# Column 0 of the attention tile: VectorE casts become ScalarE copies, and the first units are issued in another order

## The chip, the core and the metric

The kernel runs on one core of a Trainium2 chip. A core has five engines that run their own instruction queues side by side and meet at semaphores: TensorE (PE, matrix multiplies; PEld is its weight load), VectorE (DVE), ScalarE (ACT), GpSimd (POOL) and SyncE (SP, which here only issues DMA transfers). The metric is the device time of one execution in microseconds. Before the change three runs took 1192.21, 1198.12 and 1201.44 us, so the median is 1198.12 us.

## The reference, cut to what matters

```python
def mab(q, kv):                      # B, N, C = 4, 12608, 128; 32 inducing rows
    s = scale * (q @ kv.transpose(0, 2, 1))
    a = np.exp(s - s.max(-1, keepdims=True))
    a /= a.sum(-1, keepdims=True) + 1e-09
    return a @ kv
h = mab(I, x)                        # 32 rows attend to all of x
x = mab(x, h)                        # all of x attends to the 32 rows of h
x_prev = shift_by_one_row(x)         # first row zero
k = np.maximum((mu_k*x + (1-mu_k)*x_prev) @ w_k, 0.0)       # d_ff = 1024
r = sigmoid((mu_r*x + (1-mu_r)*x_prev) @ w_r)
out = r * (k*k @ w_v)
```

The shift by one row is what the change touches: every stretch of tokens needs the last token of the stretch before it.

## The kernel before, in words

Each of the 4 batches is cut into 6 blocks of 2048 tokens and a tail of 320. A block is 4 groups of 512 tokens. The expensive part, the channel mix, runs in **units**: one group has 4 units, each of 256 of the 1024 hidden columns, so there are 400 units in all. A unit is

- `up` (L882, PE): six matmuls of R (attention weights of the group) with W into a bank pair `ps_a`, of which there are two;
- `square` (L892, DVE): the relu out of `ps_a` into `k_t`; then L900 and L901 (ACT): the square, once rounded into `kh`, once in full into `k_t`; then L904 (POOL): `kl` = the rest;
- `down` (L916, PE): six matmuls of kh and kl with the two halves of w_v, issued four units behind its `up`.

The main loop takes two units at a time. At the group's end DVE multiplies by the gate (L921) and transposes (L931), and SP stores. `zgate` (L865, PE) and L868 (ACT) compute the gate.

The attention is woven in between the units. A table of events (`at(n, f)`, run at the end of the loop step that holds unit n; `soon(n, f)` runs earlier, between the `up`s and the squares of that step) says what is issued when, and that order is the order of every engine's queue. `stage_a` of the next batch: scores (L406, PE, bank `pb_a`), its maximum and exponential, `hmm` (L473, PE, also into `pb_a`) and `acc` (L486 or L488, DVE), which empties `pb_a`; the next block's scores can only be written into `pb_a` when acc has read it. `stage_b` of the next block of this batch: scores (L640, PE), a softmax on DVE and ACT, and its result as a high and a low part in the tile `ahl` (128 partitions x 2 x 513): `high` is L680 (ACT), `low` is L683 (DVE). `ahl` has four strips of 32 partitions, one per group; column 0 of a strip must hold the last column of the strip before it. That is `joins`: three copies of 32x2 elements from `ahl` itself (L693) and one from the R of the previous block (L695; at a batch's first block it is a memset, L697). `spread` (L706 and L707, SP) then copies `ahl` by DMA into four R tiles, and waits for joins. There are 23 such blocks (a batch's tail has no joins, and the first block of batch 0 is made otherwise). Two of them, the second block of batch 0 and the first of batch 1, are on a shorter schedule (`quick`).

The first block of batch 0 goes group by group in `start`: softmax parts (`sc`, `tu`, `mx`, `df`, `ex`, `nm`), then `high` (`hi0` to `hi3`: ACT L812) and `put` (`put0` to `put3`): transposes on PE (L817), the high part on ACT (L823), the low part on DVE (L824), then the copy of rows 0 to 31 to rows 32 to 63, one column on. For group 0 that copy is two casts on ACT and two on DVE (L829); for groups 1 to 3 it is a POOL memset (L832) and two SP DMAs (L834) and two small ones for column 0 (L620), which need the previous group's R and the L834 pair. The parts of units 3 to 8 are held back to named steps by `finish`.

Of the kernel before, what the change touches and what calls it, by code (L numbers as in the profile page):

```python
# [8 lines left out]
F32 = mybir.dt.float32  # L9
# [10 lines left out]
def kernel(  # L20
# [11 lines left out]
    nc = tc.nc  # L32
    B, N, C = x.shape
    M = inducing.shape[0]
    F = w_k.shape[1]
    P = 128
    Q = 4
    FC = F // P
    G = 512
# [24 lines left out]
    HP = P // 2  # L64
# [557 lines left out]
    def stage_b(b, j, at, t, quick=False):  # L622
# [3 lines left out]
        S = batches[b]  # L626
# [55 lines left out]
        def low():  # L682
            nc.vector.tensor_tensor(out=L["a"][:, 1, 1:w + 1], in0=L["aT"],  # L683
                                    in1=L["a"].bitcast(F32)[:, 0, 1:w + 1], op=ALU.subtract)
            if full:
                joins()

        def joins():
            A = L["a"]
            for i in range(Q):  # L690
                dst = A[M * i:M * (i + 1), :, 0:1]
                if i > 0:
                    nc.vector.tensor_copy(out=dst, in_=A.bitcast(F32)[M * (i - 1):M * i, :, G:])  # L693
                elif j > 0:
                    nc.vector.tensor_copy(out=dst, in_=S.R[j * Q - 1].bitcast(F32)[:M, :, G - 1:G])  # L695
                else:
                    nc.vector.memset(dst.bitcast(F32), 0.0)  # L697

# [46 lines left out]
        at(t + 6, back)  # L745
        at(t + 7, high)
        at(t + 9, low)
        for i in range(Q):
            at(t + 10 + i, lambda i=i: spread(i))

    def stage_b_head(gs):
# [3 lines left out]
        S = batches[0]  # L755
# [50 lines left out]
        def place(k):  # L806
            g = gs[k]
            X = {}

            def high():  # L810
                X["a"] = scratch[:, g % 2].rearrange("p (k q m) -> p k q m", k=Q, q=Q)
                nc.scalar.copy(out=X["a"], in_=L["q", k].unsqueeze(2).broadcast_to([P, Q, Q, M]))  # L812

            def put():
                ps = pb_tile("a")
                for c in range(Q):
                    nc.tensor.transpose(out=ps[:, c * P:(c + 1) * P], identity=ident,  # L817
                                        in_=X["a"][:, c].rearrange("p q m -> p (q m)"))
                rows(S, g)
                R = S.R[g]  # L820
                src = ps.rearrange("r (s p) -> r p s", p=M)
                hi, lo = (R[:, x, :G].rearrange("r (p s) -> r p s", p=M) for x in range(2))
                nc.scalar.copy(out=hi, in_=src)  # L823
                nc.vector.tensor_tensor(out=lo, in0=src, in1=hi.bitcast(F32), op=ALU.subtract)  # L824
                if g == 0:
                    halo(S, g)
                    for x, copy in enumerate((nc.scalar.copy, nc.vector.tensor_copy)):
                        for p in (0, HP):
                            copy(out=R[p + M:p + 2 * M, x, 1:G], in_=R.bitcast(F32)[p:p + M, x, :G - 1])  # L829
                    return  # L830
                flat = R.bitcast(F32).rearrange("p x g -> p (x g)")
                nc.gpsimd.memset(flat[:, G:G + 1], 0.0)  # L832
                for p in (0, HP):
                    nc.sync.dma_start(out=flat[p + M:p + 2 * M, 1:2 * G + 1], in_=flat[p:p + M, :2 * G])  # L834
                halo(S, g)
            return high, put
# [118 lines left out]
    def finish(n):  # L955
        return lambda: run(held.pop(n))
# [172 lines left out]
    def at(n, f, place=1):  # L1129
        events.setdefault(n, ([], [], []))[place].append(f)  # L1130
# [4 lines left out]
    def start():  # L1135

        part0, pl0 = stage_b_head([0, 1])
        part1, pl1 = stage_b_head([2, 3])
        sc0, tu0, mx0, df0, ex0, nm0 = part0([0])
        sc1, tu1, mx1, df1, ex1, nm1 = part0([1])  # L1140
        sc2, tu2, mx2, df2, ex2, nm2 = part1([0, 1])
        (hi0, put0), (hi1, put1) = pl0

        def bank():
            return pv.tile([P, G], F32, name="ps_v")

        wa, wb, wg = (wpart(c, bank) for c in (0, 1, None))
        assert F // G == 2
        S = batches[0]
        scores_1, settle_1, home_1 = sooner[2:]  # L1150
        rexp, rman, rsign, rjoin = conv["r", 0]
        run([sc0, gates, rexp, sc1, tu0, mx0, df0, ex0, wa[0], scores_1, tu1, nm0, wa[1],
             hi0, wa[2], rman, mx1, df1, rsign, rjoin, put0, ex1, wb[0], wb[1], wg[0], settle_1, wg[1],
             *vlow, nm1, wb[2], hi1])
        for n, f in ((0, wg[2]), (1, put1), (1, sc2)):
            soon(n, f)
        (hi2, put2), (hi3, put3) = pl1
        for n, f in ((1, tu2), (1, mx2), (1, df2), (1, ex2), (1, home_1), (2, nm2), (2, hi2), (2, hi3),
                     (3, finish(3)), (4, finish(4)), (5, finish(5)), (5, put2)):
            at(n, f)  # L1160
        soon(4, lambda: units[0][0].gate_tile())
        for f in (lambda: units[0][0].zgate(first=True, hold=sig), lambda: run(reversed(sig)),
                  finish(6), finish(7)):
            at(7, f, 0)
        at(7, put3)
# [87 lines left out]
```

## Time and profile before

| what | value |
|---|---|
| profiled execution, its own time | 1201.99 us |
| span, first to last instruction | 1199.1 us, mean granted TensorE clock 0.958 |
| busy PE / DVE / ACT / POOL | 1100.9 / 1011.2 / 913.1 / 955.6 us |
| L904 POOL, kl | x399, 935.7 us |
| L892 DVE, k_t | x400, 465.5 us |
| L693 + L695 DVE, joins | x69 + x20, 92.6 + 43.0 us |

The span is what the trace covers; 2.9 us of the execution lie outside it. Busy times of engines overlap, so their sum says nothing; what counts is where PE stands still and on whom it waits. The granted clock is 1.00 where TensorE runs at 2.4 GHz throughout and 0.5 where it runs at 1.2 GHz, the two levels it has.

### The profile page before, as it was taken

Reading aid. Unit: us, or ns where it says so; the run is one execution under the profiler, and the core shown is the slowest. Engines: PE = TensorE matmul, PEld = TensorE weight load, DVE = VectorE, ACT = ScalarE, POOL = GpSimd, SP = SyncE. Lnnn points to the kernel's source line nnn. Section 1 sums busy time; section 2 is a strip of 40 time slices with the busy share of each in tenths; the row PEclk is TensorE's granted clock in tenths of the full one; section 3 lists DMA queues with packets and bytes.
Section 4 is the critical chain, followed back from the end, with each engine's and each line's share of the span. In section 5 each row is a group of like instructions: output and inputs, shape, how many; then the busy total and the mean of one; then the engine's idle time right before and its main releaser. Section 6 shows DMA issues by size and latency. Waiting matters only on the chain.

```text
span 1199.1 us, 18674 instructions
## 1 busy us (share of the span) xinstructions
PE 1100.9 (92%) x6493; PEld 759.7 (63%) x6493; DVE 1011.2 (84%) x1343; ACT 913.1 (76%) x1065; POOL 955.6 (80%) x431
## 2 busy tenths in 40 slices
PE   8789889889999988989999889988999999998998
PEld 6466556557676655657666557655766766666776
DVE  7869999887799989987688999998768798898765
ACT  7677677668787776767887677865887888787896
POOL 4378678679888876877887778866988889898997
PEclk9899899889999989999999999998999999998999
DMA  8118557764156687575117567785322345444122
GB/s 327 45 53 199 126 128 176 186 155 86 18 118 161 150 193 176 138 184 122 32 20 173 141 154 171 176 194 135 74 33 40 77 88 106 89 96 93 34 39 39
DMA packets 250973, 142.22 MB, mean 119 GB/s; under 512 B 220000, under 2 KB 221184, under 8 KB 248576
## 3 DMA queue, kind: packets, MB, share of 16 engines
q1 hardware_dynamic: 248048, 140.68, 51.2%
q8 instruction: 51, 0.84, 0.3%
q10 hardware_dynamic: 2832, 0.36, 0.2%
q14 instruction: 42, 0.34, 0.1%
HBM read 45.89 MB, written 43.65 MB: 75 GB/s over the span
## 4 chain that ended last, share of the span: by engine, by line
PE 66%; DVE 21%; issue 5%; DMA 3%; ACT 3%; SPq 1%; POOL 1%; DVEq 0%; ACTq 0%; POOLq 0%
PE ps_v L916 34%; PE ps_a L882 22%; DVE k_t L892 8%; PE ps_v L865 4%; DVE ahl L695 2%; DVE xs L370 2%; DVE ahl L693 2%; PE pb_a L406 2%; DVE oT L921 1%; ACT kh L900 1%; PE pb_a L473 1%; DVE ot L931 1%; DMA xt<-xd 1%; DMA R<-R 1%; ACT k_t L901 1%
## 5 line engine op out<-in xcount | busy, mean ns | idle before, releaser
L904 POOL TENSOR_TENSOR kl<-k_t,kh 128x1024 fp32r<-128x1024 f32 (+1 forms) x399 | 935.7, 2377 | 212.2 <-ACT k_t L901 190.0
L892 DVE TENSOR_SCALAR k_t<-ps_a 128x1024 f32<-128x1024 f32 (+1 forms) x400 | 465.5, 1197 | 68.4 <-PE ps_a L882 67.6
L900 ACT ACTIVATE kh<-k_t 128x1024 fp32r<-128x1024 f32 (+1 forms) x375 | 388.9, 1037 | 162.1 <-DVE k_t L892 122.4
L901 ACT ACTIVATE k_t<-k_t 128x1024 f32<-128x1024 f32 (+1 forms) x400 | 419.1, 1048 | 45.8 <-DVE kh L897 33.8
L882 PE MATMUL ps_a<-R,W 64*128 64x512 f32 (+1 forms) x2400 | 358.3, 428 | 31.6 <-DVE k_t L892 24.9
L882 PEld LDWEIGHTS ps_a<-R,W 64*128 64x128 f32 x2400 | 222.9, 195 | 160.2 <-issue 68.5
L916 PE MATMUL ps_v<-kh,wvh 128*128 128x512 f32 (+1 forms) x800 | 259.7, 406 | 0.0
L916 PE MATMUL ps_v<-kh,wvl 128*128 128x512 f32 (+1 forms) x800 | 247.5, 391 | 0.0
L916 PE MATMUL ps_v<-kl,wvh 128*128 128x512 f32 (+1 forms) x800 | 244.9, 387 | 0.0
L916 PEld LDWEIGHTS ps_v<-kh,wvh 128*128 128x128 f32 x800 | 144.7, 191 | 61.8 <-issue 18.6
L916 PEld LDWEIGHTS ps_v<-kh,wvl 128*128 128x128 f32 x800 | 151.2, 190 | 32.8
L916 PEld LDWEIGHTS ps_v<-kl,wvh 128*128 128x128 f32 x800 | 150.6, 189 | 32.2
L868 ACT ACTIVATE rT<-ps_v 128x512 f32<-128x512 f32 (+1 forms) x99 | 57.8, 584 | 51.8 <-PE ps_v L865 51.8
L921 DVE SCALAR_TENSOR_TENSOR oT<-rT,ps_v 128x512 f32<-128x512 f32 (+1 forms) x100 | 66.4, 664 | 34.9 <-PE ps_v L916 34.3
L693 DVE CAST ahl<-ahl 32x2 fp32r<-32x2 f32 x69 | 92.6, 1342 | 1.7
L865 PE MATMUL ps_v<-R,W 128*128 128x512 f32 (+1 forms) x198 | 76.5, 469 | 0.0
L406 PE MATMUL pb_a<-xt,indT 128*32 128x512 f32 x112 | 23.0, 909 | 53.4 <-DVE acc L488 38.9
L931 DVE STREAM_TRANSPOSE ot<-oT 128x512 f32<-128x512 f32 (+1 forms) x100 | 69.1, 691 | 0.1
L865 PEld LDWEIGHTS ps_v<-R,W 128*128 128x128 f32 x198 | 31.9, 203 | 38.9 <-issue 38.9
L370 DVE STREAM_TRANSPOSE xs<-xb 128x512 f32<-128x512 f32 x68 | 45.5, 688 | 0.2
L695 DVE CAST ahl<-R 32x2 fp32r<-32x2 f32 x20 | 43.0, 2149 | 0.0
L406 PEld LDWEIGHTS pb_a<-xt,indT 128*32 128x32 f32 x112 | 2.7, 126 | 63.4 <-DVE acc L488 45.0
(215 smaller groups left out, 555.7 us busy)
## 6 DMA issues: line engine op xcount, KB each, us to landing
R<-ahl SPq DMA_DIRECT2D x184, 128.2 KB, 2.6
R<-ahl SPq DMA_DIRECT2D x184, 128.1 KB, 2.5
out_dram<-ot SPq DMA_DIRECT2D x184, 128.0 KB, 3.5
xb<-in_x_dram SPq DMA_DIRECT2D x18, 1024.0 KB, 8.5
xd<-xs SPq DMA_DIRECT2D x34, 512.0 KB, 3.2
xt<-xd SPq DMA_DIRECT2D x68, 256.0 KB, 5.4
kh<-in_x_dram SPq DMA_DIRECT2D x4, 512.0 KB, 6.2
kl<-in_x_dram SPq DMA_DIRECT2D x4, 512.0 KB, 9.5
```

Of the source, the lines that this page charges most:

```text
L370: nc.vector.transpose(out=xs.rearrange("p (s q) -> p s q", q=M), in_=S.xb[j][:, :, M * c:M * (c + 1)])
L693: nc.vector.tensor_copy(out=dst, in_=A.bitcast(F32)[M * (i - 1):M * i, :, G:])
L695: nc.vector.tensor_copy(out=dst, in_=S.R[j * Q - 1].bitcast(F32)[:M, :, G - 1:G])
L865: nc.tensor.matmul(out=ps[:, :w], lhsT=S.W[0][:, F:WF], rhs=R[:, x, :w], start=(x == 0), stop=(x == 1))
L882: nc.tensor.matmul(out=ps[:, c, :w], lhsT=S.W[wt][hs, cs], rhs=R[hs, x, :w], start=(n == 0), stop=(n == 2))
L892: nc.vector.tensor_scalar(out=k, in0=ps[:, :, :w], scalar1=0.0, scalar2=None, op0=ALU.max)
L900: nc.scalar.activation(out=kh, in_=k, func=AF.Square)
L901: nc.scalar.activation(out=k, in_=k, func=AF.Square)
L904: eng.tensor_tensor(out=kl[:, :, a:z], in0=k[:, :, a:z], in1=kh.bitcast(F32)[:, :, a:z], op=ALU.subtract)
L916: nc.tensor.matmul(out=self.v, lhsT=wt[:, fc, :], rhs=kk[:, c, :], start=(fc == 0 and n == 0), stop=(fc == FC - 1 and n == 2))
L921: nc.vector.scalar_tensor_tensor(out=self.oT, in0=self.rT, scalar=1.0, in1=self.v, op0=ALU.add, op1=ALU.mult)
L931: nc.vector.transpose(out=ot[:, o:o + w], in_=self.oT)
```

## The change

Four edits.

1. `joins` uses `nc.scalar.copy` instead of `nc.vector.tensor_copy`, and on the full blocks that are not `quick` it is issued one event later than `low` (on `quick` blocks still right behind it). The memset stays on DVE.
2. `put0`: the copy of the low part of group 0 by one column becomes two SP DMAs instead of two DVE casts. The high part stays on ACT.
3. `start`: put1 moves from ahead of the squares of units 0 and 1 to behind them; the scores of groups 2 and 3 (`sc2`) and their softmax move from step 0 to step 2.
4. `nm2` and `hi2` move from step 2 to step 4, `hi3` to step 5, put2 ahead of `finish(5)`.

```diff
-            if full:
+            if full and quick:
                 joins()
@@ joins
-                    nc.vector.tensor_copy(out=dst, in_=A.bitcast(F32)[M * (i - 1):M * i, :, G:])
+                    nc.scalar.copy(out=dst, in_=A.bitcast(F32)[M * (i - 1):M * i, :, G:])
                 elif j > 0:
-                    nc.vector.tensor_copy(out=dst, in_=S.R[j * Q - 1].bitcast(F32)[:M, :, G - 1:G])
+                    nc.scalar.copy(out=dst, in_=S.R[j * Q - 1].bitcast(F32)[:M, :, G - 1:G])
@@ stage_b
         at(t + 9, low)
+        if full:
+            at(t + 10, joins)
@@ put, g == 0
-                    for x, copy in enumerate((nc.scalar.copy, nc.vector.tensor_copy)):
-                        for p in (0, HP):
-                            copy(out=R[p + M:p + 2 * M, x, 1:G], in_=R.bitcast(F32)[p:p + M, x, :G - 1])
+                    for p in (0, HP):
+                        nc.scalar.copy(out=R[p + M:p + 2 * M, 0, 1:G], in_=R.bitcast(F32)[p:p + M, 0, :G - 1])
+                        nc.sync.dma_start(out=R.bitcast(F32)[p + M:p + 2 * M, 1, 1:G],
+                                          in_=R.bitcast(F32)[p:p + M, 1, :G - 1])
@@ start
-        for n, f in ((0, wg[2]), (1, put1), (1, sc2)):
+        for n, f in ((0, wg[2]), (2, sc2), (4, nm2), (4, hi2)):
             soon(n, f)
-        for n, f in ((1, tu2), (1, mx2), (1, df2), (1, ex2), (1, home_1), (2, nm2), (2, hi2), (2, hi3),
-                     (3, finish(3)), (4, finish(4)), (5, finish(5)), (5, put2)):
+        for n, f in ((1, put1), (1, home_1), (2, tu2), (2, mx2), (2, df2), (2, ex2),
+                     (3, finish(3)), (4, finish(4)), (5, put2), (5, finish(5)), (5, hi3)):
             at(n, f)
```

The changed file's line numbers are 2 or 3 higher than those of before behind `spread` (L693, L695, L706 and L707 keep theirs): L892 there is L895, L900 and L901 are L903 and L904, L904 (POOL) is L907, L921 is L924, L931 is L934, L832 is L835.

On DVE, at the end of the second block of batch 0, before:

```order
L931 STREAM_TRANSPOSE ot<-oT 128x512
L683 TENSOR_TENSOR ahl<-pb_b,ahl 128x512
L695 CAST ahl<-R 32x2
L693 CAST ahl<-ahl 32x2 x3
L892 TENSOR_SCALAR k_t<-ps_a 128x1024 x2
L370 STREAM_TRANSPOSE xs<-xb 128x512 x2
```

and on DVE at the same place after the change:

```order
L934 STREAM_TRANSPOSE ot<-oT 128x512
L683 TENSOR_TENSOR ahl<-pb_b,ahl 128x512
L895 TENSOR_SCALAR k_t<-ps_a 128x1024 x2
L370 STREAM_TRANSPOSE xs<-xb 128x512 x2
L924 SCALAR_TENSOR_TENSOR oT<-rT,ps_v 128x512
```

The four casts between the subtraction (L683) and the next two relus are gone from DVE's queue. On ACT at that place after the change:

```order
L903 ACTIVATE kh<-k_t 128x1024
L904 ACTIVATE k_t<-k_t 128x1024
L695 CAST ahl<-R 32x2
L693 CAST ahl<-ahl 32x2 x3
L871 ACTIVATE rT<-ps_v 128x512
L903 ACTIVATE kh<-k_t 128x1024
```

They stand there behind a unit's two squares and ahead of the gate's tanh (L871, before L868) and the next squares.

On POOL at the start of the unit loop (kl of units 0, 1, ... and the memsets of put1, put2 and put3), before:

```order
L179 TENSOR_TENSOR wvl<-ot,wvh 128x512 x2
L832 MEMSET R 128x1
L904 TENSOR_TENSOR kl<-k_t,kh 128x1024 x6
L832 MEMSET R 128x1
L904 TENSOR_TENSOR kl<-k_t,kh 128x1024 x2
L832 MEMSET R 128x1
```

and on POOL after the change:

```order
L179 TENSOR_TENSOR wvl<-ot,wvh 128x512 x2
L907 TENSOR_TENSOR kl<-k_t,kh 128x1024 x2
L835 MEMSET R 128x1
L907 TENSOR_TENSOR kl<-k_t,kh 128x1024 x3
L835 MEMSET R 128x1
L907 TENSOR_TENSOR kl<-k_t,kh 128x1024 x3
```

The first memset, on which put1's DMAs wait, now stands behind the kl of units 0 and 1; the second stands behind five kl instead of six.

## Rows read from the trace of the kernel before

**Rows 1.** First part of the page: busy time, share of span, instructions.
```profile
PE 1100.9 (92%) x6493; PEld 759.7 (63%) x6493; DVE 1011.2 (84%) x1343; ACT 913.1 (76%) x1065; POOL 955.6 (80%) x431
```

**Rows 2.** Waits of PE: who waited for whom, us in total, times, longest.
```profile
PE pb_a L406 <- DVE acc L488: 38.9, 9, 5.6
PE ps_a L882 <- DVE k_t L892: 24.9, 16, 3.2
PE pb_a L406 <- DVE acc L486: 14.5, 3, 4.9
```

**Rows 3.** Groups of instructions by line and form: busy us, mean ns, idle before.
```profile
L892 DVE TENSOR_SCALAR k_t<-ps_a 128x1024 f32<-128x1024 f32 x384 | 453.1, 1213 | 66.4 <-PE ps_a L882 65.7
...
L693 DVE CAST ahl<-ahl 32x2 fp32r<-32x2 f32 x69 | 92.6, 1342 | 1.7
...
L695 DVE CAST ahl<-R 32x2 fp32r<-32x2 f32 x20 | 43.0, 2149 | 0.0
...
L440 ACT ACTIVATE alpha<-mkr 128x1 f32<-128x1 f32 x15 | 4.2, 277 | 0.0
```

**Rows 4.** Instructions on tile R, 40 to 90 us: ns min/median/max, first and last start.
```profile
L829 ACT CAST R<-R x2: 612/614/617, 43.3 to 43.9; 32x511 fp32r<-32x511 f32 x2
...
L829 DVE CAST R<-R x2: 1234/1328/1423, 43.5 to 44.8; 32x511 fp32r<-32x511 f32 x2
```

**Rows 5.** Timeline of one block's end: start, us, engine, line, count, idle before.
```profile
449.81 1.83 DVE L695 CAST ahl<-R 32x2 fp32r<-32x2 f32 x1
...
451.68 4.91 DVE L693 CAST ahl<-ahl 32x2 fp32r<-32x2 f32 x3
...
451.82 4.74 POOL L904 TENSOR_TENSOR kl<-k_t,kh 128x1024 fp32r<-128x1024 f32 x2 [0.20 <-PE ps_a L882]
...
456.29 1.04 PE L640 MATMUL pb_b<-xt,hT 128*32 128x512 f32 x8
...
459.71 1.06 ACT L900 ACTIVATE kh<-k_t 128x1024 fp32r<-128x1024 f32 x1 [5.98 <-DVE k_t L892]
...
461.88 0.31 DVE L488 SCALAR_TENSOR_TENSOR acc<-acc,alpha,pb_a 128x128 f32<-128x128 f32 x1
...
462.24 1.57 PE L406 MATMUL pb_a<-xt,indT 128*32 128x512 f32 x8 [4.91 <-DVE acc L488]
```

**Rows 6.** Windows from joins to joins: length, busy PE PEld DVE ACT POOL, clock.
```profile
127.72:166.70 38.98, 34.16 (x200) 22.71 (x199) 35.45 (x46) 26.91 (x32) 28.59 (x13) 0.91 0.62 149
...
488.10:522.46 34.36, 31.82 (x200) 21.69 (x199) 32.78 (x45) 26.92 (x32) 28.58 (x13) 1.00 0.78 182
...
778.05:816.28 38.23, 33.35 (x200) 22.23 (x199) 35.20 (x46) 26.92 (x32) 28.57 (x13) 0.96 0.77 170
...
995.88:1025.66 29.78, 29.78 (x160) 20.70 (x159) 25.82 (x33) 26.20 (x29) 28.24 (x13) 1.00 0.55 107
1025.66:1059.45 33.79, 31.61 (x160) 21.59 (x159) 30.30 (x34) 26.08 (x29) 28.82 (x13) 0.95 0.39 78
```

**Rows 7.** Timeline of the first units, 36 to 75 us.
```profile
45.82 0.10 POOL L832 MEMSET R<- 128x1 f32 x1
...
46.25 2.07 PE L882 MATMUL ps_a<-R,W 64*128 64x512 f32 x7 [0.93 <-DVE R L829]
...
50.80 1.25 SPq L834 DMA_DIRECT2D R<-R  x2
...
51.99 0.96 PE L882 MATMUL ps_a<-R,W 64*128 64x512 f32 x6 [1.91 <-DVE k_t L892]
...
55.98 3.18 PE L882 MATMUL ps_a<-R,W 64*128 64x512 f32 x12 [1.21 <-DMA R<-R]
...
72.97 0.47 PE L882 MATMUL ps_a<-R,W 64*128 64x512 f32 x1 [2.97 <-DMA R<-R]
```

**Rows 8.** Timeline behind the first joins, 96 to 98 us.
```profile
96.94 1.47 PE L882 MATMUL ps_a<-R,W 64*128 64x512 f32 x5 [2.58 <-DVE k_t L892]
...
97.30 0.82 PEld L882 LDWEIGHTS ps_a<-R,W 64*128 64x128 f32 x5 [0.17 <-DMA R<-ahl]
```

More of the change, by code (lines that the diff above doesn't have):

```diff
@@ L1142, in start @@
         (hi0, put0), (hi1, put1) = pl0
+        (hi2, put2), (hi3, put3) = pl1
         def bank():
@@ L1154, in start @@
              *vlow, nm1, wb[2], hi1])
-        for n, f in ((0, wg[2]), (1, put1), (1, sc2)):
+        for n, f in ((0, wg[2]), (2, sc2), (4, nm2), (4, hi2)):
             soon(n, f)
-        (hi2, put2), (hi3, put3) = pl1
-        for n, f in ((1, tu2), (1, mx2), (1, df2), (1, ex2), (1, home_1), (2, nm2), (2, hi2), (2, hi3),
-                     (3, finish(3)), (4, finish(4)), (5, finish(5)), (5, put2)):
+        for n, f in ((1, put1), (1, home_1), (2, tu2), (2, mx2), (2, df2), (2, ex2),
+                     (3, finish(3)), (4, finish(4)), (5, put2), (5, finish(5)), (5, hi3)):
             at(n, f)
```

## The prediction

> **What bounds the kernel now.** I read the shares of busy time first: PE is busy for 1100.9 of 1199.1 us [rows 1], so 98 us of standing still is what can be won from PE directly, besides what it loses by running slowly. Next, the waits of PE: 53.4 us are waits of the scores L406 for DVE's acc (12 times, 38.9 + 14.5) and 24.9 us are waits of `up` for DVE's relu [rows 2]. So DVE, although it is busy less than PE, is what PE waits for, at some twenty places. The third view is the groups of instructions: the casts of joins move 64 numbers per strip and take 1342 and 2149 ns [rows 3], more than the relu of 128x1024 at 1213 ns. A cast of 32x2 cannot need that; it must be waiting inside.
>
> The timeline of one block says for what [rows 5]. DVE's four casts run from 449.81 to 456.59 us. The three of L693 take 4.91 us while POOL does two kl back to back, 451.82 to 456.56, and the last cast ends 0.03 us behind the second kl. A cast gets through only between two POOL instructions. Behind the casts DVE does not rest until acc at 461.88 (456.59 to 461.88 is 5.3 us of transposes, gate and two relus). PE has finished the scores L640 at 457.33 and stands for 4.91 us before L406; ACT has stood for 5.98 us. This picture comes back, larger or smaller, in nearly every one of the 23 blocks, and the windows show the price [rows 6]: the block of 34.36 us, where the casts met POOL less, against 38.98 and 38.23 us for the same work.
>
> A second price is in the clock. In the window with 34.36 us the granted clock is 1.00 (2.4 GHz) and PE is busy for 31.82 us; with the same 199 or 200 pieces of PE work it is busy for 34.16 us at 0.91 and 33.35 at 0.96 [rows 6]. After a stand of 4 to 5 us PE runs its next matmuls at 1.2 GHz, and the same work takes 1.5 to 2.3 us longer.
>
> **The change, part by part.** *Joins to ScalarE.* 89 casts leave DVE, 92.6 + 43.0 = 135.6 us [rows 3], 5.9 us per block. What does a copy of 32x2 cost on ACT? No row has it. The nearest for size is ACT's 128x1 at 277 ns [rows 3]. Whether ACT also waits for POOL is shown by one pair of rows, the two halves of the same copy of 32x511 at the same time, with POOL at work: on ACT 612 to 617 ns, on DVE 1234 to 1423 [rows 4]. The ACT numbers don't scatter, so I take 0.28 us, four copies 1.1 us; the upper bound is the DVE price, 5.9 us per block. ACT is busy for 26.9 us of a block [rows 6] and would be at 28.0 of some 32: room enough.
>
> The Trainium skill ("SBUF — State Buffer", Who interferes with whom) says that a DVE cast in its two-port mode takes a port pair that it shares with GpSimd, as a lock for a whole instruction, and that ACT never waits on anyone; the trace agrees on both sides [rows 4, 5]. Against the change stands the skill's "Perfetto Trace Analysis" (Optimizing Scalar/DVE Operations): where DVE has a fast mode, DVE is quicker than ScalarE. By that rule alone the move would only add ACT's 1.1 us per block; the mean of 1342 ns [rows 3] says that here it doesn't hold, and it is priced below as a rival.
>
> What is late once the casts are gone? In rows 5 DVE would reach acc at 449.81 + 5.3 = 455.1 us, before PE's hmm has ended (where L640 begins, 456.29, and a little), so acc would run at about 456.5 to 456.8 and L406 could follow L640 at 457.33. The whole 4.9 us go, with some 1.5 us to spare. The longest of these waits is 5.6 us [rows 2], still under the 6.7 us that four long casts take. The relus that `up` waits for (longest 3.2 us [rows 2]) stand directly behind the casts, so they come earlier by the casts' full length.
>
> So the stands that go: 53.4 us of acc, and of the 24.9 us of relu all but 1.91 us in the first units [rows 7] and the 2.58 us behind the first joins [rows 8]. That one stays: the R of unit 16 is also only just there (the weight load waits for the DMA of ahl at 97.30 [rows 8]), and its DMAs start when the first copy is done, which ACT reaches about when DVE did. 53.4 + 20.4 = **73.8 us**.
>
> The clock: seven windows of the kind of 127.72 to 166.70 (first and last in rows 6) are busy for 14.5 us more than 7 x 31.82. Three blocks at a batch's end have no clean window; I give them the seven's mean, 2.07, so 6.2. Three blocks of batch 3 with a stand take 31.61 - 29.78 = 1.8 each [rows 6], 5.5. Three blocks at or just behind a batch's beginning, at clocks of the 0.96 kind, 33.35 - 31.82 = 1.5 each, 4.6. Together **30.8 us**; three blocks stood for some 2.5 us without losing the clock and count nothing. As bounds: 20 us if half the slow matmuls have another cause, 38 if all 16 cost what the first window of rows 6 cost (2.34).
>
> *The low part of group 0 by DMA.* DVE loses two casts of 1.3 us [rows 4]; PE waited for them until 46.25 us [rows 7]. The first DMA can start when the last of the low part is written, 43.3 us, the second 0.6 us later, and a copy of this kind lands 2.6 us after its start (two in a row, 50.80 to 55.98 [rows 7]): 45.9 and 46.5 us. They are ahead of L834 in SP's queue, which is empty then. Cost 0, between -0.3 and +0.5.
>
> *The new order at the start* speaks against the change. put1's DMAs need its memset, which ran at 45.82 us before any kl [rows 7]; now it stands behind the kl of units 0 and 1. Unit 0's matmuls end at about 46.7 (two of the seven from 46.25 on), DVE is free for its relu at 47.0, so 48.2; two squares at 1.06 us [rows 5] give 50.4, two kl at 2.37 [rows 5] 55.1, the memset 55.2. From L834 to `up` of unit 4 it was 50.80 to 55.98, 5.2 us [rows 7]; so 60.4 instead of 55.98, **4.4 us later**. Then the second stand, 2.97 us for the R of group 2 [rows 7], whose memset waited for six kl and now for five, shrinks or goes, with the slow clock behind it. Against this, the R of group 3 needs units 6 and 7, which are late by then, and I count up to 2 us for it. I take +3 us, between -2 and +8.
>
> **The sum.** 1201.99 - 73.8 - 30.8 + 0 + 3 = 1100.4 us, against the profiled execution. That stands 0.32% above the median of the runs, so the prediction for the median is 1100.4 x 1198.12 / 1201.99 = **1097 us**.
>
> **The rivals.**
>
> *The wait only moves.* With DVE out of the way, PE meets the next engine. POOL needs 28.6 us of every block and DVE 28.4 without casts (32.78 less 4.4, or 35.20 less 6.8); ACT 28.0; PE itself 31.8 [rows 6]. All fit, but with an eighth to spare, and each is a queue in order. For it: the DMA traffic of a block is pressed into 32 us instead of 38. Against it: the windows 488.10 to 522.46 and 995.88 to 1025.66 run at full clock, the second with PE busy for 29.78 of 29.78 us and POOL for 28.24 [rows 6], and nothing new waits. If half of the 105 us comes back, 1149 us.
>
> *The change doesn't do what it says*, because the copies wait for POOL on ACT as well. Then ACT has 26.9 + 5.9 to 6.7 = up to 33.6 us per block and PE follows: 1.8 us for 19 blocks, 34 us, so about 1131. Against it: rows 4.
>
> *Slower.* ScalarE is on the path and VectorE's wait was not: L406 would have waited as long for what follows the casts, and 1.1 us of copies stand ahead of a tanh and two squares in 23 blocks. That gives 25 + 3 us more, 1226. It decides if the stand at acc shrinks by less than 1.2 us per block when the casts go. Against it: DVE has no idle time between the casts and acc [rows 5]. The rule of the Trainium skill on DVE's fast mode ("Perfetto Trace Analysis", above) comes to this case.
>
> **How the numbers follow.** I give the forecast 0.78, the wait that moves 0.13, copies that wait too 0.06, slower 0.03. The forecast's own range is 1084 (clock term 38, start -2) to 1112 (clock term 20, start +8); the copies that wait too give 1131. The range 1084 to 1135 takes in both and leaves out the half that comes back and the slower case, 0.16. About 1% is what a measurement of this kernel can tell from no change; all cases but the last lie far more than that below 1198, with a little kept for a mix of them that cancels: faster 0.95, same 0.02, slower 0.03.
>
> **What would show it.** Right: L693 and L695 on ACT at 0.2 to 0.3 us each without scatter; hardly a wait of L406 for acc left and waits of `up` for the relu below 8 us in total; windows from joins to joins of about 32 us (30 in batch 3) at clock 1.00; POOL idle before kl lower by a good half; `up` of unit 4 at about 60 us. Wrong: copies of over 1 us on ACT (they wait too); L406 or `down` waiting for ACT or POOL instead (moved); the clock below 1.00 in blocks without a stand (then that term was mine, not the stands'); PE standing beyond 62 us for R of group 1 (the start costs more).

## The result, and the profile after

| | before | after |
|---|---|---|
| median of the runs timed side by side (us) | 1199.38 (4 runs, 1192.21 to 1201.44) | 1096.77 (4 runs, 1096.19 to 1097.10) |
| ratio after / before | | 0.9154, 95% interval 0.9114 to 0.9193 |
| profiled execution (us) | 1201.99 | 1096.45 |
| its span (us) | 1199.1 | 1094.7 |
| PE not busy in the span (us) | 98.2 | 31.8 |
| mean granted clock of PE | 0.958 | 0.993 |

The change makes the kernel 8.5% faster; 1097 us was predicted. Line numbers below are those of the kernel that a row belongs to; three lines were added to the kernel ahead of `up`, so L882, L892 and L904 of before are L885, L895 and L907 of after.

The page of after, busy time by engine (us, share of span, instructions), and from its groups the one of kl (busy us, mean ns, idle before and who ended most of it); [rows 1] of before:

```profile
PE 1062.9 (97%) x6493; PEld 741.0 (68%) x6493; DVE 875.4 (80%) x1252; ACT 929.3 (85%) x1154; POOL 955.3 (87%) x431
...
L907 POOL TENSOR_TENSOR kl<-k_t,kh 128x1024 fp32r<-128x1024 f32 (+1 forms) x399 | 936.3, 2378 | 106.8 <-ACT k_t L904 83.4
```

PE is busy 97% of a shorter span, and with the same 6493 instructions for 38 us less: it runs faster. DVE lost 135.8 us, what its casts took in [rows 3]. The waits of PE in after (who for whom, us in total, times, longest), against [rows 2]:

```profile
PE ps_a L885 <- DMA R<-R: 8.4, 1, 8.4
PE ps_a L885 <- DVE k_t L895: 3.1, 5, 2.1
...
PE pb_a L406 <- DVE acc L488: 0.9, 3, 0.3
```

The 53.4 us for acc are 0.9 us, the 24.9 us for the relu are 3.1 us. The largest wait left is a single one of 8.4 us, in the first units. POOL's idle time ahead of kl, 212.2 us in the page of before, is halved (106.8). The two lines of casts, now on ACT (count; ns min/median/max, first and last start):

```profile
L693 ACT CAST ahl<-ahl x69: 190/193/197, 99.3 to 995.4; 32x2 fp32r<-32x2 f32 x69
...
L695 ACT CAST ahl<-R x20: 172/176/178, 99.1 to 994.8; 32x2 fp32r<-32x2 f32 x20
```

They scatter by 7 ns. On DVE the same two lines had means of 1342 and 2149 ns [rows 3]. Windows from joins to joins in after (length, then busy time and count of PE, PEld, DVE, ACT, POOL, granted clock, DMA share, GB/s), one of the usual kind, one across a batch's end, one of batch 3. Joins come every twelve units in the usual case, so the first and the third hold twelve units; below, such a stretch is called a block:

```profile
169.53:201.14 31.61, 31.60 (x200) 21.69 (x199) 28.55 (x41) 27.58 (x36) 28.59 (x13) 1.00 0.89 200
...
482.57:580.08 97.51, 96.26 (x612) 67.41 (x611) 73.99 (x112) 82.35 (x100) 85.65 (x37) 1.00 0.39 84
...
905.51:935.29 29.78, 29.78 (x160) 20.70 (x159) 23.93 (x29) 26.88 (x34) 28.58 (x13) 1.00 0.55 107
```

From the second joins on, every one of the 21 windows is at clock 1.00, with PE busy all but 1.3 us of it or less. The nine of about 200 pieces of PE work are 31.60 to 31.93 us long (34.33 to 39.61 before), those of batch 3 all 29.7 to 29.8. One block's end in after, the counterpart of [rows 5] (start, us, engine, line, count, idle before):

```profile
450.97 0.18 ACT L695 CAST ahl<-R 32x2 fp32r<-32x2 f32 x1
...
451.17 0.62 ACT L693 CAST ahl<-ahl 32x2 fp32r<-32x2 f32 x3
...
453.66 1.04 PE L640 MATMUL pb_b<-xt,hT 128*32 128x512 f32 x8
...
453.91 0.35 DVE L488 SCALAR_TENSOR_TENSOR acc<-acc,alpha,pb_a 128x128 f32<-128x128 f32 x1 [1.05 <-PE pb_a L473]
...
454.10 4.74 POOL L907 TENSOR_TENSOR kl<-k_t,kh 128x1024 fp32r<-128x1024 f32 x2 [0.19 <-ACT k_t L904]
454.52 1.04 PE L406 MATMUL pb_a<-xt,indT 128*32 128x512 f32 x8
```

Four copies take 0.82 us. Now DVE waits for PE's hmm (1.05 us) before acc, and L406 follows L640 without a gap.

### The profile page after: what moved, and what is told of

Its sections match the earlier page's. It is cut to its first block, busy times and chain, and to the rows that moved or that the text cites. A ratio compares the mean times of both kernels' runs of the same rounds, so it can differ in the third digit from the quotient of the medians.

```text
span 1094.7 us, 18706 instructions
## 1 busy us (share of the span) xinstructions
PE 1062.9 (97%) x6493; PEld 741.0 (68%) x6493; DVE 875.4 (80%) x1252; ACT 929.3 (85%) x1154; POOL 955.3 (87%) x431
## 4 chain that ended last, share of the span: by engine, by line
PE 91%; DVE 4%; DMA 2%; ACT 2%; issue 1%; POOL 0%; SPq 0%; DVEq 0%; ACTq 0%; POOLq 0%
PE ps_v L919 50%; PE ps_a L885 28%; PE ps_v L868 6%; PE pb_b L640 2%; PE pb_a L473 2%; DVE k_t L895 1%; PE pb_a L406 1%; DMA k_t<-in_moe_w_v_dram 1%; DMA kh<-in_x_dram 1%; PE pb_a L582 1%; POOL kl L907 0%; ACT k_t L904 0%; ACT kh L903 0%; DMA R<-R 0%; PE pb_b L406 0%
## 5 line engine op out<-in xcount | busy, mean ns | idle before, releaser
L907 POOL TENSOR_TENSOR kl<-k_t,kh 128x1024 fp32r<-128x1024 f32 (+1 forms) x399 | 936.3, 2378 | 106.8 <-ACT k_t L904 83.4
L895 DVE TENSOR_SCALAR k_t<-ps_a 128x1024 f32<-128x1024 f32 (+1 forms) x400 | 465.2, 1198 | 73.8 <-PE ps_a L885 68.2
L904 ACT ACTIVATE k_t<-k_t 128x1024 f32<-128x1024 f32 (+1 forms) x400 | 419.3, 1048 | 48.0 <-DVE kh L900 36.0
L903 ACT ACTIVATE kh<-k_t 128x1024 fp32r<-128x1024 f32 (+1 forms) x375 | 389.1, 1038 | 58.0 <-PE ps_v L919 38.6
L885 PE MATMUL ps_a<-R,W 64*128 64x512 f32 (+1 forms) x2400 | 340.3, 411 | 17.4 <-DMA R<-R 8.4
L885 PEld LDWEIGHTS ps_a<-R,W 64*128 64x128 f32 x2400 | 211.7, 186 | 136.7 <-issue 63.0
L919 PEld LDWEIGHTS ps_v<-kl,wvh 128*128 128x128 f32 x800 | 149.8, 188 | 31.8
L924 DVE SCALAR_TENSOR_TENSOR oT<-rT,ps_v 128x512 f32<-128x512 f32 (+1 forms) x100 | 66.5, 665 | 36.3 <-PE ps_v L919 36.0
L871 ACT ACTIVATE rT<-ps_v 128x512 f32<-128x512 f32 (+1 forms) x99 | 57.9, 585 | 33.1 <-PE ps_v L868 32.6
L868 PE MATMUL ps_v<-R,W 128*128 128x512 f32 (+1 forms) x198 | 71.9, 444 | 0.0
L934 DVE STREAM_TRANSPOSE ot<-oT 128x512 f32<-128x512 f32 (+1 forms) x100 | 69.2, 692 | 0.1
L868 PEld LDWEIGHTS ps_v<-R,W 128*128 128x128 f32 x198 | 29.4, 188 | 35.7 <-issue 35.7
L647 DVE STREAM_TRANSPOSE s<-pb_b 128x512 f32<-128x512 f32 (+1 forms) x27 | 17.6, 652 | 26.2 <-PE pb_b L640 26.1
L900 DVE SCALAR_TENSOR_TENSOR kh<-ps_a,k_t 128x1024 fp32r<-128x1024 f32 x25 | 30.6, 1224 | 4.3 <-PE ps_v L919 2.1
L640 PE MATMUL pb_b<-xt,hT 128*32 128x512 f32 x184 | 24.3, 600 | 0.0
L473 PE MATMUL pb_a<-xb,e 128*32 128x128 f32 x576 | 19.5, 276 | 0.0
```

What stands on the lines that cost most here:

```text
L640: nc.tensor.matmul(out=ps[M * i:M * (i + 1), :w], lhsT=S.hT, rhs=rhs, start=True, stop=True)
L868: nc.tensor.matmul(out=ps[:, :w], lhsT=S.W[0][:, F:WF], rhs=R[:, x, :w], start=(x == 0), stop=(x == 1))
L871: nc.scalar.activation(out=self.rT, in_=ps[:, :w], func=AF.Tanh, scale=0.5)
L885: nc.tensor.matmul(out=ps[:, c, :w], lhsT=S.W[wt][hs, cs], rhs=R[hs, x, :w], start=(n == 0), stop=(n == 2))
L895: nc.vector.tensor_scalar(out=k, in0=ps[:, :, :w], scalar1=0.0, scalar2=None, op0=ALU.max)
L903: nc.scalar.activation(out=kh, in_=k, func=AF.Square)
```

## The experiments

Eleven kernels, in three groups. The kernel before was timed beside each group, and a ratio is to the runs of its own group: a median of 1197.54 us (13 runs, 1191.31 to 1203.60) for the copies alone, the rest alone and the first two kernels on VectorE; 1200.61 us (13 runs, 1192.96 to 1205.93) for the low part, put1's place, eight copies and the memsets; 1202.69 us (3 runs, 1202.21 to 1204.41) for the other three.

### Which part of the change does it

**The copies alone.** The kernel before with the first part of the diff only (copies on ACT, a step behind `low`); the low part of group 0 and the order of the first units as before:

```diff
-            if full:
+            if full and quick:
                 joins()
@@ in joins, both lines
-                    nc.vector.tensor_copy(out=dst, ...
+                    nc.scalar.copy(out=dst, ...
@@ behind at(t + 9, low)
+        if full:
+            at(t + 10, joins)
```

> The kernel before with the first edit alone: the copies of joins on ScalarE, one event later; the start as before. If the whole gain is the copies, the trace of after says what remains: from the first down behind the first joins to the end the changed kernel is 110.7 us shorter than before (988.4 against 1099.1), and up to there 6.3 us longer (106.3 against 100.0). So this kernel should take some 1201 - 110 = 1090 to 1093 us, 4 to 6 us less than the changed one, with L693 and L695 at 0.18 to 0.20 us each. Rival: the new start is a part of the gain (it brings units 0 to 3 forward); then this kernel is slower than the changed one, 1098 us or more.

1090.02 us (1088.98 to 1090.36), ratio 0.9098 [0.9051, 0.9145]. The copies are the whole gain. The rest of the change costs 1096.77 - 1090.02 = 6.7 us; the runs of the two kernels don't overlap. The traces say the same without a comparison of two groups of runs. Windows from the start of the 21st kl to the end, before, after, and the copies alone (columns as above):

```profile
115.03:1199.10 1084.07, 1002.20 (x5749) 691.45 (x5745) 922.28 (x1163) 831.21 (x946) 888.20 (x379) 0.96 0.52 115
```

```profile
121.39:1094.66 973.27, 964.81 (x5749) 675.32 (x5745) 793.70 (x1078) 846.15 (x1031) 888.92 (x379) 1.00 0.58 128
```

```profile
113.69:1086.94 973.25, 964.73 (x5749) 675.39 (x5745) 793.65 (x1078) 846.14 (x1031) 889.07 (x379) 1.00 0.58 129
```

With the same 5749 pieces of PE work, both kernels gain 110.8 us there, and all that they differ by lies ahead of it, in the first units.

**The rest alone.** After, with the copies back on DVE, right behind `low`:

> The changed kernel with the joins put back: casts on VectorE, right behind the subtraction; only the edits of the start are left. If the gain is the copies alone, 4 to 7 us slower than before, 1203 to 1207, with the waits of L406 for acc again near 53 us in total. Rival, the start helps: below 1198.

Its four runs took 1191.68, 1210.84, 1216.16 and 1219.69 us. They scatter too widely for a ratio, so the time decides nothing between the expectation and the rival. In the trace, of the run of 1216.16 us, PE waits for acc as before (41.2 + 14.4 us) and for the relu (26.8 us), and it has the 8.5 us stand for R of group 1. That the new start gains nothing is shown by the copies alone, above.

**The low part of group 0.** After, with the two DMAs of L831 put back as casts on DVE:

```diff
-                        nc.sync.dma_start(out=R.bitcast(F32)[p + M:p + 2 * M, 1, 1:G], ...
+                    for p in (0, HP):
+                        nc.vector.tensor_copy(out=R[p + M:p + 2 * M, 1, 1:G], ...
```

> The changed kernel with the low part of group 0 copied on VectorE again instead of by two DMAs. The prediction put this edit at 0 (-0.3 to +0.5). If so, 1096 to 1097.5; in the trace PE waits some 0.9 us for the second cast. Rival: it frees VectorE ahead of unit 0's relu, which starts the chain to the memset: then the kernel is 1 to 2 us slower than the changed one, since two casts of 1.3 us stand ahead of everything in the start.

1097.07 us (1095.98 to 1098.24), ratio 0.9152 [0.9111, 0.9193]: the same as after within the scatter of the runs.

**put1's place.** After, with put1 issued ahead of the squares again:

```diff
-        for n, f in ((0, wg[2]), (2, sc2), (4, nm2), (4, hi2)):
+        for n, f in ((0, wg[2]), (1, put1), (2, sc2), (4, nm2), (4, hi2)):
@@ and out of the list for at():  (1, put1),
```

> The changed kernel with put1 ahead of the squares of units 0 and 1 again, so that its memset stands ahead of every kl and its two casts ahead of the squares; the rest of the new start stays. If the wait of 8.45 us for the R of group 1 is what the new start costs, up of unit 4 comes at 55 to 56 us instead of 60.0 and the time is 1090 to 1093. Rival: the first unit's delay is won back anyway before unit 16 (which waits for the R of its own group), so that this changes nothing, 1095 to 1097.

1092.06 us (1091.08 to 1092.77), ratio 0.9109 [0.9069, 0.9150]: 4.7 us of the 6.7 come from the place of put1, that is of its casts and its memset together. Timeline of PE in this kernel (start, us, engine, line, count, idle before); the units 4 and 5 run at 54.95 without a wait, others stand:

```profile
51.08 2.93 PE L885 MATMUL ps_a<-R,W 64*128 64x512 f32 x12 [2.62 <-DVE k_t L895]
...
54.95 2.50 PE L885 MATMUL ps_a<-R,W 64*128 64x512 f32 x12
...
64.72 1.65 PE L885 MATMUL ps_a<-R,W 64*128 64x512 f32 x6 [2.98 <-DVE kh L900]
```

### Why the casts were dear: the engine, the step, or the shape

**On VectorE, a step later.** After, with the two lines in `joins` back on DVE, but still at step t + 10:

> The changed kernel with the four copies of joins on VectorE, but still one event behind the subtraction. If what counts is the engine that does them, as slow as the start alone: 1200 to 1207 us, casts at 1.3 to 2.1 us in the mean. Rival: what counts is the later step (spread and the casts no longer follow the subtraction at once); then a good part of the gain stays, 1100 to 1150.

1199.35 us (1193.66 to 1205.16, 8 runs), ratio 1.0025 [0.9992, 1.0057]. Nearly nothing of the gain is left, so the step behind `low` is not what brings it. It may be worth a little: this kernel has the new start too, which costs 6.7 us, so 1204 us would be no effect at all, and the waits for acc are 46.3 us (33.6 below, and 12.7 for L486) instead of 53.4. The casts and two waits of PE in this kernel (views as above):

```profile
L693 DVE CAST ahl<-ahl x69: 157/2287/2424, 99.7 to 1090.1; 32x2 fp32r<-32x2 f32 x69
...
L695 DVE CAST ahl<-R x20: 1184/1290/2408, 97.6 to 1083.0; 32x2 fp32r<-32x2 f32 x20
```

```profile
PE pb_a L406 <- DVE acc L488: 33.6, 9, 5.0
PE ps_a L885 <- DVE k_t L895: 24.7, 20, 3.2
```

One of these casts can be done in 157 ns; the median is 2287 ns, about the length of a kl (2378 ns, above). So its time is a wait for POOL. In the trace of before this holds for every one of them: its 59 casts of over 0.5 us all began while a POOL instruction ran, and ended 16 to 27 ns behind the end of one; of its 30 short casts, 157 to 165 ns, one began while POOL ran.

**On VectorE, one column at a time.** The kernel before with each 32x2 cast written as two of 32x1, nothing else:

```diff
-                    nc.vector.tensor_copy(out=dst, in_=A.bitcast(F32)[M * (i - 1):M * i, :, G:])
+                    for x in range(2):
+                        nc.vector.tensor_copy(out=A[M * i:M * (i + 1), x, 0:1],
+                                              in_=A.bitcast(F32)[M * (i - 1):M * i, x, G:])
@@ and the line for j > 0 likewise
```

> The kernel before, where each 32x2 cast of joins on VectorE is cut into two of 32x1. The theory that only the two-column form waits for POOL (a lock between the two engines that the one-column copy L428, 143 to 146 ns without scatter, doesn't need): 178 casts of about 0.15 us, 1.2 us per block on VectorE, nearly no stand of PE, 1090 to 1098 us, as good as ScalarE. Rival: any small VectorE cast into this tile waits, or VectorE is simply too full and has to be relieved of joins: then twice as many casts cost more, 1200 to 1320 us in the first case, and a gain of less than half, above 1150, in the second.

1088.27 us (1087.13 to 1088.38), ratio 0.908 [0.904, 0.912], a little below the 1090 to 1098 that I expected. Its casts, and the waits of PE:

```profile
L694 DVE CAST ahl<-ahl x138: 132/141/150, 92.5 to 983.2; 32x1 fp32r<-32x1 f32 x138
...
L698 DVE CAST ahl<-R x40: 120/124/129, 92.3 to 982.5; 32x1 fp32r<-32x1 f32 x40
```

```profile
PE ps_a L886 <- DMA R<-R: 3.5, 1, 3.5
...
PE ps_a L886 <- DVE k_t L896: 2.2, 2, 1.6
```

Twice the instructions on the same engine, on the same numbers, and none waits: 120 to 150 ns, although all 178 began while a POOL instruction ran. So it was neither VectorE as such nor the place of the casts in its queue, but the two-column form, which has to take turns with POOL. The move to ScalarE wasn't needed.

### How much room the engines have

The prediction said that ScalarE had "room enough". These kernels lengthen the burst on one engine by doing the same copies several times; they compute the same.

**ScalarE, eight times.** After, with each copy issued 8 times:

```diff
-                    nc.scalar.copy(out=dst, in_=A.bitcast(F32)[M * (i - 1):M * i, :, G:])
+                    for _ in range(8):
+                        nc.scalar.copy(out=dst, in_=A.bitcast(F32)[M * (i - 1):M * i, :, G:])
@@ and the line for j > 0 likewise
```

> The changed kernel with every copy of joins made eight times on ScalarE (the same numbers again): 28 more copies of 0.19 us per block, 5.3 us, about what the casts took on VectorE. ScalarE is busy for 27.6 of 31.6 us of a block, so it would have 32.9. If a wait in front of PE is what costs, and ScalarE's queue has the room of the units in flight, only the excess comes through, 1.3 us for the 15 blocks of that kind and nothing elsewhere: up to 20 us, 1097 to 1117. Rival (slower): ScalarE is as much on the path as VectorE was, PE stands in every block for 3 to 5 us and loses its clock: 1170 to 1200.

1189.07 us (1188.21 to 1191.12, 8 runs), ratio 0.9911 [0.9882, 0.9939]. My main expectation missed by 70 us and more; the rival, ScalarE on the path, held. But with a burst of 7.1 us ACT itself has 32.8 us of work in a block, more than PE's 31.6, so this run doesn't tell a full ACT from a wait that it causes. Two smaller doses do.

**ScalarE, three times** (the same edit with 3):

> The changed kernel with every copy of joins made three times on ScalarE: a burst of about 2.3 us per block instead of 0.8. Theory from the run with eight: what a burst anywhere ahead of kl costs is set by POOL, which needs 28.6 us of every block and stands while the burst lasts; a block of 31.6 us lets it stand for 3.0 us, a block of batch 3 (29.75 us) for 1.2 us. With 2.3 us of burst POOL stands about 1.7 us plus what it stood anyway: 0 to 0.5 us in the 15 blocks with attention for the next batch, about 1 us in the 5 of batch 3, so 1097 to 1110. Rival, ScalarE's own fill (27.6 + 1.6 = 29.2 of 31.6): no cost anywhere, 1096 to 1098.

1098.37 us (1097.68 to 1099.07), ratio 0.913 [0.9103, 0.9156]: 1.6 us more than after for 1.8 us more of ACT in most of the 23 blocks. That is within what the theory expected and 0.4 us above the rival's range, so this time alone decides nothing between them.

**ScalarE, five times** (the same edit with 5):

> The same with five: a burst of about 3.9 us. By POOL's slack the block is 28.6 + 3.2 (its stand behind the burst) + 1.4 (its other stands) = 33.2 us instead of 31.6, 1.6 us in 15 blocks, and 2 to 2.6 us in the 5 of batch 3: 35 to 40 us more, 1130 to 1140. Rival, ScalarE's own fill (27.6 + 3.1 = 30.7 of 31.6): no more than 10 us, below 1107.

1130.07 us (1129.27 to 1130.87), ratio 0.9393 [0.9366, 0.9420], where POOL's slack said 1130 to 1140. ACT is not full here. Windows from joins to joins (columns as above), of the kernels with 3, 5 and 8 copies:

```profile
419.71:451.32 31.61, 31.60 (x200) 21.72 (x199) 28.56 (x41) 29.11 (x44) 28.55 (x13) 1.00 0.77 185
```

```profile
462.17:494.90 32.73, 31.62 (x200) 21.73 (x199) 28.93 (x41) 30.44 (x52) 28.52 (x13) 1.00 0.85 198
```

```profile
451.29:486.74 35.45, 32.44 (x202) 22.09 (x201) 29.43 (x42) 32.77 (x64) 28.49 (x13) 1.00 0.70 164
```

With 5 copies no engine is busy for 32.73 us: PE 31.62, ACT 30.44, POOL 28.52. But POOL's idle time is 32.73 - 28.52 = 4.2 us, just the burst. The timeline of the same kernel shows both (start, us, engine, line, count, idle before), first POOL and then ACT:

```profile
436.15 9.65 POOL L909 TENSOR_TENSOR kl<-k_t,kh 128x1024 fp32r<-128x1024 f32 x4 [3.77 <-ACT k_t L906]
```

```profile
429.43 1.08 ACT L697 CAST ahl<-R 32x2 fp32r<-32x2 f32 x5
430.53 3.31 ACT L694 CAST ahl<-ahl 32x2 fp32r<-32x2 f32 x15
433.87 1.06 ACT L905 ACTIVATE kh<-k_t 128x1024 fp32r<-128x1024 f32 x1
```

ACT copies from 429.43 to 433.84, 4.4 us; kl needs ACT's square, so POOL stands till 436.15 and then has its kl to do back to back. Whatever time ACT takes away, POOL loses. POOL needs 28.5 us of a block and PE 31.6, so a burst of some 3.1 us fits, and beyond it the block grows by the burst: 28.5 + 4.4 = 32.9 (measured 32.73), 28.5 + 7.1 = 35.6 (measured 35.45 at clock 1.00; the other blocks of that kernel are 36.5 us at 0.95). In batch 3, where a block is 29.75 us without a burst, the rule is about 1 us too strict. With 3 copies its four blocks are like this one:

```profile
906.46:936.55 30.09, 29.95 (x160) 20.74 (x159) 24.01 (x29) 28.04 (x41) 28.43 (x13) 1.00 0.54 106
```

POOL stands for 1.7 us there with a burst of 2.6, so the block grows by 0.3 us, not by 1.3; with 8 copies it is 34.6 us, not 35.5. What gives POOL this 0.9 us stays open.

| burst on ACT per block (us) | 0.8 (after) | 2.6 | 4.4 | 7.1 |
|---|---|---|---|---|
| time (us) | 1096.8 | 1098.4 | 1130.1 | 1189.1 |

**VectorE, one column, five times.** The kernel before with 5 times the two 32x1 casts, 40 in a block, so that DVE has a long burst that waits for nobody. Is it the length alone that PE's stand at acc comes from, or does the wait for POOL cost more?

> The kernel before with one-column casts on VectorE, each made five times: 40 casts of 0.14 us, a burst of about 5.7 us per block, as long as the four casts of before (5.9 us in the mean), but without a wait for POOL inside. If only the length of the burst counts, about as slow as before, 1175 to 1200 us, with L406 waiting for acc and POOL for ACT as there. Rival: the lock itself costs, beyond the casts' length (it lines VectorE up with POOL's ends); then clearly faster than before, 1100 to 1160.

1124.04 us (1123.56 to 1124.51), ratio 0.9343 [0.9316, 0.9370]. The size that I expected was wrong, since I had reckoned with a burst of 40 x 0.141 us. The timeline of this kernel shows why, and what it did:

```profile
456.89 0.89 DVE L698 CAST ahl<-R 32x1 fp32r<-32x1 f32 x10
...
457.81 2.80 DVE L694 CAST ahl<-ahl 32x1 fp32r<-32x1 f32 x30
...
466.26 1.06 PE L406 MATMUL pb_a<-xt,indT 128*32 128x512 f32 x8 [1.76 <-DVE acc L488]
```

Casts in a row overlap: 30 in 2.80 us, one each 0.093 us, so the burst was 3.7 us. Against the same block of before [rows 5] it is 6.78 - 3.73 = 3.05 us shorter, and the stand before L406 is 4.91 - 1.76 = 3.15 us shorter. So the stand follows the burst's length one to one, behind 1.9 to 2.0 us that cost nothing. The other blocks agree: within a batch, bursts of 6.8 us in before have stands of 4.82 to 4.91 us behind them, two bursts of 4.4 to 4.5 us have 2.5, and those of 3.7 us here have 1.75 to 1.85; in the last block of a batch only 1.2 us are free (6.79 and 5.56, 3.72 and 2.50). That the long casts were waits adds nothing. By the number alone the result falls in the rival's range, but it comes from the shorter burst, not from a cost of the wait itself.

### A version that beats both

One column at a time on VectorE, as above, and the memsets that put1 to put3 need on POOL issued ahead of the first kl:

```diff
+            def clear():
+                rows(S, g)
+                nc.gpsimd.memset(S.R[g].bitcast(F32)[:, 0, G:G + 1], 0.0)
...
-                nc.gpsimd.memset(flat[:, G:G + 1], 0.0)
...
-             *vlow, nm1, wb[2], hi1])
+             *vlow, nm1, wb[2], hi1, clear1, pl1[0][2], pl1[1][2]])
```

> The kernel before with one-column casts on VectorE (as the run above) and with the three memsets of put1 to put3 issued together ahead of the first kl; the order of the start is that of before. put2's DMAs then wait only for its subtraction (about 65.7 us) and not for a memset behind six kl (68.6 us). If the wait of 3.5 us for the R of group 2 is the memset's, it shrinks to about 0.5 us, and with it goes some slow clock: 1083 to 1086 us. Rival: the wait is the DMAs' own length (two in a row, 5.2 us): nothing changes, 1088.

1086.58 us (1085.71 to 1086.87), ratio 0.9062 [0.9014, 0.9110]: 10.2 us below after, and 0.6 above the range that I expected. The windows from the 21st kl to the end, of the one-column form alone and of this kernel, are

```profile
113.13:1086.30 973.17, 964.50 (x5749) 675.22 (x5745) 808.68 (x1248) 831.89 (x946) 887.82 (x379) 1.00 0.58 129
```

```profile
111.16:1084.74 973.58, 964.92 (x5749) 675.35 (x5745) 808.83 (x1248) 831.95 (x946) 887.92 (x379) 1.00 0.58 129
```

against 973.27 us of after and 973.25 of the copies alone: from there on ScalarE and the one-column form are worth the same. What this kernel gains, it gains in the first units: it reaches its 21st kl at 111.16 us, after at 121.39, the copies alone at 113.69 and the one-column form alone at 113.13. So most of the 10.2 us is the old order of the first units, and the memsets bring 2.0 us in these traces. The time of the one-column form alone is 1.75 us below that of the copies alone, but by these windows the difference lies ahead of the 21st kl and is not a gain of the form. In the timeline of PE the stand for R of group 2, 3.5 us with the one-column form alone, has become

```profile
70.29 0.46 PE L890 MATMUL ps_a<-R,W 64*128 64x512 f32 x1 [0.55 <-DMA R<-R]
70.94 1.63 PE L890 MATMUL ps_a<-R,W 64*128 64x512 f32 x11 [0.18 <-DMA R<-R]
```

## Why the prediction was right, and where its terms were off

I cut both spans at the first `down` behind the first joins: 100.04 us in before, 106.33 in after. Behind that cut lies all that the copies do. Windows on both sides of about that place (columns as above), before and then after:

```profile
42.55:100.04 57.49, 46.70 (x227) 31.93 (x226) 44.53 (x60) 38.64 (x48) 37.35 (x22) 0.86 0.26 72
100.04:1199.10 1099.06, 1017.19 (x5826) 701.87 (x5825) 936.00 (x1183) 844.13 (x961) 901.69 (x385) 0.96 0.53 117
```

```profile
43.25:105.63 62.38, 45.03 (x226) 29.54 (x226) 37.59 (x54) 40.88 (x53) 39.10 (x23) 0.90 0.24 66
105.63:1094.70 989.07, 980.57 (x5828) 685.84 (x5826) 807.33 (x1098) 857.98 (x1044) 900.42 (x384) 1.00 0.59 130
```

Behind the cut before took 1099.06 us, after 1094.7 - 106.33 = 988.37: 110.7 us less. PE's busy time falls by 1017.2 - 980.0 = 37.2 us of it (980.57 less some 0.6 us ahead of the cut), the time in which it stands by the other 73.5 us. In front of the cut after is 6.3 us longer.

| term of the sum | predicted | measured |
|---|---|---|
| stands of PE | -73.8 | -73.5 |
| slow clock | -30.8 | -37.2 |
| low part by DMA | 0 | 0 (0.3, within the scatter) |
| new order at the start | +3 | +5.6, and 0.7 ahead of it |

**The stands** were right, in size and cause. Nothing took their place: from the second joins on no window keeps more than 1.3 us in which PE isn't busy. The 2.58 us behind the first joins [rows 8], which I left standing, did stay in substance, as 0.95 and 0.82 us for the DMA of ahl:

```profile
102.36 0.47 PE L885 MATMUL ps_a<-R,W 64*128 64x512 f32 x1 [0.95 <-DMA R<-ahl]
103.65 2.75 PE L885 MATMUL ps_a<-R,W 64*128 64x512 f32 x11 [0.82 <-DMA R<-ahl]
```

**The clock term** had the right cause and was 6.4 us too small, though inside its bounds (20 to 38). The windows say where. The nine windows of about 200 pieces lose 16.1 us of PE's busy time against the 14.5 that I counted, because 31.82 us, which I took for the clean block, was not quite clean: it is 31.6 now. The three windows across a batch's end had no clean counterpart in the trace, and I gave each the others' mean of 2.07 us; they lose 9.7 together, not 6.2. One of them, in before, is

```profile
522.46:628.02 105.56, 99.18 (x612) 68.76 (x611) 81.86 (x118) 82.06 (x96) 85.80 (x37) 0.97 0.36 76
```

against 96.26 us busy in after (window above). Batch 3 loses 3.7 in its four windows, which hold two of the three blocks that I counted at 1.8 each; the beginnings of batches lose 5.4 instead of 4.6. The remaining 2.4 us lie before the first of these windows and behind the last, where the third block of batch 3 has its stand (3.23 us in before, up to 1098.65).

**The start** was mis-sized too. The step on `up` of unit 4 was right: it ran at 59.99 us, and 60.4 was predicted. Timeline of the first units in after, the counterpart of [rows 7]:

```profile
43.97 1.24 SPq L831 DMA_DIRECT2D R<-R  x2
...
48.87 0.96 PE L885 MATMUL ps_a<-R,W 64*128 64x512 f32 x6 [0.41 <-DVE k_t L895]
...
51.07 4.66 POOL L907 TENSOR_TENSOR kl<-k_t,kh 128x1024 fp32r<-128x1024 f32 x2 [4.67 <-ACT k_t L904]
...
53.54 0.69 DVE L826 TENSOR_TENSOR R<-pb_a,R 128x512 fp32r<-128x512 f32 x1 [3.59 <-ACT R L825]
...
55.66 0.10 POOL L835 MEMSET R<- 128x1 f32 x1
55.79 1.14 SPq L837 DMA_DIRECT2D R<-R  x2
...
59.99 3.62 PE L885 MATMUL ps_a<-R,W 64*128 64x512 f32 x12 [8.45 <-DMA R<-R]
```

The memset stands behind two kl, as worked out (55.66 us, predicted 55.2), the DMAs follow, and PE stands for 8.45 us. The prediction laid all of the delay on the memset. But the DMAs need the subtraction L826 as well, and its operand is a cast of ACT that now stands behind the squares; L826 ends at 54.23 us. A memset ahead of the kl would have brought the DMAs forward from 55.79 us to 54.23 at best, by some 1.5 us. I then took only +3 of the 4.4 us, and hoped that the shrinking second stand would pay for the rest. It did go: there is no stand for R of group 2 in after. But stands of 1.72, 2.06 and 0.84 us at 70.89, 83.95 and 90.30 us came instead. The range (-2 to +8) held it, and put1 ahead of the squares shows that 4.7 us hang on put1's place.

**The total** is nearer than its terms, and that is luck. A clock term 6.4 us too small and a start 2.6 us too cheap, with 0.7 us ahead of it, nearly cancel: 6.4 - 3.3 = 3.1 us, and 1100.4 predicted less 3.1 is 1097.3, against 1096.45 of the profiled execution. The 0.8 us left over are less time around the span, 1096.45 - 1094.7 = 1.75 us instead of 2.9, less the 0.3 us by which the stands were too large.

**The price of a copy on ACT** was 0.19 us (0.21 in a row), not 0.28; ACT has 27.6 us of a block, not 28.0.

**"ACT would be at 28.0 of some 32: room enough"** was the weak sentence, though it did no harm here. Busy time said 4 us of room; the runs with more copies show some 3.1 in the usual block, set by POOL, which waits for ACT's squares and can't catch up. A VectorE burst has 1.9 us in the same block, where I reckoned "some 1.5 us to spare" for acc.

**The rivals.** The wait that moves (1149 us) is refuted for this change, and exists: at 7.1 us of copies the kernel is at 1189 us, with PE waiting 32.3 us for DVE's kh and 26.5 us for ACT's rT. Copies that wait on ACT too (1131) are refuted by the 172 to 197 ns. Slower (1226), by the 0.9 us left for acc. The rule that spoke against the change, the Trainium skill's "Perfetto Trace Analysis" (Optimizing Scalar/DVE Operations), doesn't hold where POOL is at work: 1342 and 2149 ns on DVE [rows 3], 193 and 176 on ACT.

What makes the difference between 32x2 and 32x1 no row tells directly; the rows show 157 to 2424 ns for the one and 120 to 150 for the other. The Trainium skill ("VectorE: DVE Perf Modes", What auto-detection actually checks) says that the mode with two ports is taken for a single source where it and the destination are in SBUF and their outermost counts above one are both even, or equal. By that, as I read it, 32x2 takes the mode, and 32x1, which has no such count, doesn't. The runs agree with it; they tried no other count.

## What to carry to other kernels

A tiny instruction whose duration scatters up to the length of another engine's instruction is waiting inside, and its shape or its engine can be changed; try the shape first, it may cost nothing else. Whether an engine has room for more is not read from its busy share, but from the engine behind it in the chain: a burst in an in-order queue starves that one for the whole burst, so a first estimate of the room is the block's length less the work of the busiest engine downstream (3.1 us here, right in the usual block and 0.9 us too low in batch 3). And when work moves behind other work, look at what waits for it: put1 behind the squares and kl of two units cost 4.7 us here.

## What the runs showed of the hardware that was not expected

- A DVE cast of 32x1 took 120 to 150 ns beside POOL at work; one of 32x2 took 157 to 165 ns where it didn't wait, and up to 7135 ns where it did (before, one L695). Casts of 32x1 in a row start each 0.093 us, while one lasts 0.141 us. Copies of 32x2 on ACT don't overlap so: three in 0.62 us, at 0.19 us each.
- A stand of 1.76 us before L406 left the granted clock at 1.00: its eight matmuls then took 1.06 us, as without a stand (1.04). Behind 4.91 us they took 1.57 us [rows 5]. In between it isn't settled: behind 2.49 and 2.50 us, in the kernel with 40 casts in a block, they took 1.94 us, while three blocks of before stood for some 2.5 us and kept the clock.
- The stands of 73.5 us that went brought 37.2 us more through the clock, half as much again.
